# A wider search for the priorities that order the dense stage of an attention, feed-forward and mixture-of-experts kernel

## The chip, the cores and the metric

The kernel runs on one core of a Trainium2 chip. The metric is the device time of one execution in microseconds (us); the figure for a kernel is the median of its runs.

## What is computed

Attention over pooled keys and values, a dense feed-forward layer on its output, and a layer of eight experts that takes each token to one of them or past them all. Cut to what matters:

```python
k_p = k.reshape(B, H, Sp, pool, D).mean(axis=3)          # 8 batches, 8 heads, 576 tokens, 64 wide, pool 8
v_p = v.reshape(B, H, Sp, pool, D).mean(axis=3)
scores = scale * q @ k_p.T; attn = softmax(scores); x = attn @ v_p    # as 4608 tokens x 512
h = x @ w_in; g = h * (1 / (1 + exp(-h))); x = g @ w_out              # 512 -> 2048 -> 512
do_compute = x @ w_skip > 0
e_idx = argmax(x[do_compute] @ w_gate); gate_w = its softmax value
y = gate_w * (relu(xc @ w1[e]) @ w2[e])                               # 512 -> 1024 -> 512, per expert
out[do_compute] = xc + y
```

## The kernel before

The program has two stages on one core. The **dense stage** (`dense`) does attention, the feed-forward layer and the routing for 36 tiles of 128 tokens, in 18 chunks of 256 (j = 0 to 17). Its work is cut into operations with short names, each a few instructions on one engine. For one chunk they are:

- `mm1(j, f)`, f = 0 to 15: 12 matrix products into `psh` (lines 324 to 326); then `th` (tanh on ACT, line 331), `sw` (DVE, line 337), `gh` (ACT, line 341) and `gl` (POOL or DVE, line 346), which make the two halves of the activated block; then `mm2(j, f)`: 6 products into `pso` (lines 356 to 358).
- `ev(j, t)`: `pso` to the SBUF tile `x` (line 365), and `st`: that tile to the output and to the scratch tensor `x2d` (line 371), by SP's queue.
- `dot`: 9 per tile, 18 per chunk, on DVE (line 376): the scores of eight experts and of the skip. `ra` (lines 389 to 397), `rp` (two small products into `psr`, lines 404 and 405), `re`, `rg` (lines 413 to 420) and `rb` (lines 429 to 437) turn them into list positions, `rs` (POOL, line 440) scatters the rows of one tile into the lists in DRAM. `rb` of a chunk needs that of the chunk before.

For chunk 17 the dots and the routing are not in the dense stage but in the next. The dense stage also prepares the **expert stage**, by operations that stand once: `ft` (line 829 on, the first tile's expert and list position, from the counts up to chunk 15), `fi` (line 913, SP reads the first 256 list rows), `l1` and `l2` (line 928, SP loads the first expert's W1 into `room` and W2 into `wb`, four pieces of 512 KB each; `wb` holds the router's weights until the last dot), `ga` (line 962, POOL gathers the 256 tokens from `x2d` by two indirect transfers), `xp` (line 973, PE turns them), `xq` and `xr` (lines 979 and 983, their two halves), `s1h` and `s1l`, `s2h` and `s2l` (lines 944 and 948, the two halves of a quarter of W1 or W2; the first of each pair on ACT, the second on DVE or POOL), `ti` and `tc` (small tables).

The **expert stage** (`experts`) starts with the first 256 listed tokens, whatever comes of chunk 17: eight groups of 12 products into `p` (lines 997 to 999), between which stand the turning of chunk 17's tiles (line 1052), their scores (`psl`, line 1062) and the routing of chunk 17; then products with W2 into `pys` (from line 1036), and then a chain of blocks of up to 256 tokens with its own loads and splits. Its order is written out in the program.

The dense stage's order is not. `schedule` builds it by list scheduling: every operation has a cost per engine, the operations that it needs, and a height, which is its cost plus the largest height of those that need it plus a bonus:

```python
bonus += bonus_of.get(name[0], {}).get(phase(*name), 0.0)
height[n] = min(ops[n][0].values()) + ops[n][4] + max((SIGNAL + height[u] for u in users[n]), default=0)
(_, t, t1, u), n = max((c for c in can if c[0][1] <= t0), key=lambda c: height[c[1]])
```

Of the operations that could start first, the one with the greatest height is issued next, on the engine whose end plus a penalty (`FIRST`, `LATER`, `KEEP`) is earliest. `bonus_of` is a table by kind of operation and phase: 0 to 3 for chunk 0, 1, 2 and later ones, 8 for the last chunk but one, 9 for the last. Every engine runs its instructions in the order in which they were issued.

Of the kernel before, what the change touches and what calls it, by code (L numbers as in the profile page):

```python
# [52 lines left out]
def body(tc, const, q, k, v, w_in, w_out, w_skip, w_gate, w_r, w1, w2, out, x2d, lst, base, nch, nxt):  # L53
# [3 lines left out]
    with ExitStack() as ctx:  # L57
# [392 lines left out]
        def dense():  # L450
            ops, last, st = {}, {}, {}
            bonus_of = {
# [27 lines left out]
            }  # L480
            by_tile = ("q", "sc", "mx", "ex", "ns", "nr", "pt", "pc", "pv", "xh", "xl", "dot")
            by_chunk = ("mm1", "th", "sw", "gh", "gl", "mm2", "ev", "st", "ra", "rp", "re", "rg", "rb", "rs")
# [159 lines left out]
            if nxt:  # L642
# [19 lines left out]
                for c in (0, 1, 2):  # L662
                    op(("s2h", c), {"A": 1.0}, lambda e, c=c: split_hi(S2, W2h, c), [("l2",), ("mm1", z, 2 * c + 9)])
                    op(("s2l", c), {"V": 1.2, "G": 2.45}, lambda e, c=c: split_lo(S2, W2h, W2l, c, e), [("s2h", c)])
            schedule(ops, last)

        def schedule(ops, last):
            unit = {"T": nc.tensor, "A": nc.scalar, "V": nc.vector, "G": nc.gpsimd, "S": nc.sync}
            room_for = dict(a=2, h=2, o=2 * TPC, x2=4, t=2, gh=3, gl=3, tr=2, kv=3, q=2)
            SHARED, APART = ("ns", "mix", "or", "lo", "nr", "vsum", "vput", "gl", "dot", "kput"), ("rs", "ga", "setup", "ti")  # L670
            FIRST = {"V": 0.786439, "G": 0, "A": 0.394171}
            LATER = {"V": 1.58663, "G": 0, "A": -0.769199}
            FILL, HOLD, KEEP = 181.563, 0.9, 0.6
            SIGNAL, SAME, ISSUE, REACH, COLD, IDLE, WARM = 0.135, 0.05, 0.45, 2.0, 1.8, 3.4, 4.0

            def gap(a, b):
# [22 lines left out]
            def earliest(n):  # L699
# [13 lines left out]
                for u, c in cost.items():  # L713
# [17 lines left out]
                    if len(cost) > 1:  # L731
                        more += (LATER if t > FILL else FIRST).get(u, 0.0)
                    if best is None or t + c + more < best[0]:
# [41 lines left out]
        def tiny(shape, dt=F32, parts=1, src="r"):  # L775
            n = 1
            for d in shape:
                n *= d
            o = small[src]
            small[src] = o + n  # L780
            t = (wb if src == "w" else room)[0:parts, o:o + n]
            if dt != F32:
                t = t.bitcast(dt)
            names = "abcd"[:len(shape)]
            return t.rearrange(f"p ({' '.join(names)}) -> p {' '.join(names)}",
                               **{x: d for x, d in zip(names, shape)})
# [10 lines left out]
        ex = tiny([NXP + 1, 1])  # L797
# [408 lines left out]
        with tc.manual_schedule():  # L1206
            setup()
            dense()
            if nxt:
                experts()  # L1210
# [52 lines left out]
```

## Time and profile before

| | before |
|---|---|
| median of 3 runs | 1345.49 us (1344.15 to 1347.27) |
| profiled execution, its own time | 1348.03 us |
| its span, first to last instruction | 1346.3 us |
| mean granted TensorE clock | 0.98 |
| busy: PE, DVE, ACT, POOL | 1270.8, 792.9, 568.6, 580.4 us |

PE runs the matrix products and is busy for 94% of the span. "Busy" of PE is modelled: products overlap, so a row's duration is longer than the distance to the next row. The rest of the profiled execution's time (1348.03 less 1346.3) lies around the span.

### The profile page before, as it was taken

The numbers are of one execution on the slowest core, as the hardware profiler recorded it, in microseconds if no ns is written. First come the engines' busy times: TensorE is split into PE (matmuls) and PEld (weight loads), VectorE is DVE, ScalarE is ACT, GpSimd is POOL, SyncE is SP. The second block draws the span as 40 slices with busy tenths as digits, with TensorE's granted clock in tenths as the row PEclk, the third lists the DMA queues.
The fourth block names the chain that finished last, engine by engine and source line by source line (L and its number), as shares of the span: only waits on it lengthen the run. The fifth ranks groups of instructions, "written<-read, shape, count | busy, mean of one in ns | idle before, by whom it ended". The sixth has DMA issues, their size and how long they took to land. (4 is left out here: it accounts for less than half of the span.)

```text
span 1346.3 us, 24483 instructions
## 1 busy us (share of the span) xinstructions
PE 1270.8 (94%) x8508; PEld 1132.8 (84%) x8508; DVE 792.9 (59%) x2011; ACT 568.6 (42%) x1619; POOL 580.4 (43%) x644
## 2 busy tenths in 40 slices
PE   4999999999999999999999999999559999999895
PEld 3889898898889898888888989989459999999674
DVE  7997782564837647557467547492473222333785
ACT  5876533444344444444444434433131121223573
POOL 3456355345635632663563323422271212133664
PEclk9999999999999999999999999999869999999998
DMA  7653502111301201121111101100141111426661
GB/s 244 203 197 128 198 27 61 40 40 35 92 17 62 88 9 48 58 62 48 58 35 48 40 9 40 40 33 1 45 160 48 58 40 56 166 86 251 235 240 36
DMA packets 51311, 113.84 MB, mean 85 GB/s; under 512 B 12311, under 2 KB 13335, under 8 KB 51024
## 3 DMA queue, kind: packets, MB, share of 16 engines
q1 hardware_dynamic: 44960, 96.39, 21.5%
q0 software_dynamic: 6192, 15.49, 3.5%
q8 instruction: 80, 1.31, 0.4%
q14 instruction: 79, 0.65, 0.2%
HBM read 134.58 MB, written 26.62 MB: 120 GB/s over the span
## 5 line engine op out<-in xcount | busy, mean ns | idle before, releaser
L346 POOL TENSOR_TENSOR gl<-t,gh 128x256 fp32r<-128x256 f32 x278 | 224.8, 809 | 351.9 <-ACT gh L341 247.8
L324 PE MATMUL psh<-xh,w_hi 128*128 128x256 f32 x1152 | 332.3, 288 | 1.9 <-DVE t L337 1.7
L325 PE MATMUL psh<-xl,w_hi 128*128 128x256 f32 x1152 | 323.5, 281 | 0.0
L326 PE MATMUL psh<-xh,w_lo 128*128 128x256 f32 x1152 | 323.0, 280 | 0.0
L376 DVE SCALAR_TENSOR_TENSOR junk<-x,wb 128x512 bf16<-128x512 f32 x306 | 254.7, 832 | 14.8 <-ACT x L365 9.3
L337 DVE SCALAR_TENSOR_TENSOR t<-t,psh 128x256 f32<-128x256 f32 x288 | 119.8, 416 | 210.7 <-ACT t L331 209.9
L356 PE MATMUL pso<-v_hi,gh 128*128 128x512 f32 x576 | 232.7, 404 | 0.0
L324 PEld LDWEIGHTS psh<-xh,w_hi 128*128 128x128 f32 x1152 | 217.8, 189 | 16.0 <-issue 4.7
L358 PE MATMUL pso<-v_hi,gl 128*128 128x512 f32 x576 | 225.1, 391 | 2.0 <-POOL gl L346 2.0
L357 PE MATMUL pso<-v_lo,gh 128*128 128x512 f32 x576 | 226.3, 393 | 0.0
L325 PEld LDWEIGHTS psh<-xl,w_hi 128*128 128x128 f32 x1152 | 217.7, 189 | 7.1
L326 PEld LDWEIGHTS psh<-xh,w_lo 128*128 128x128 f32 x1152 | 217.6, 189 | 0.0
L331 ACT ACTIVATE t<-psh 128x256 f32<-128x256 f32 x288 | 110.9, 385 | 224.8 <-PE psh L326 197.0
L341 ACT CAST gh<-t 128x256 fp32r<-128x256 f32 x288 | 117.0, 407 | 161.5 <-DVE t L337 140.1
L358 PEld LDWEIGHTS pso<-v_hi,gl 128*128 128x128 f32 x576 | 108.2, 188 | 28.1 <-POOL gl L346 2.5
L356 PEld LDWEIGHTS pso<-v_hi,gh 128*128 128x128 f32 x576 | 108.1, 188 | 14.6 <-issue 0.5
L357 PEld LDWEIGHTS pso<-v_lo,gh 128*128 128x128 f32 x576 | 108.4, 188 | 13.1
L1000 ACT ACTIVATE v_hi<-p 128x256 fp32r<-128x256 f32 x88 | 33.5, 384 | 185.8 <-PE p L999 177.5
L274 ACT ACTIVATE room<-pss,mx 128x72 f32<-128x72 f32 x288 | 88.2, 319 | 53.4 <-DVE mx L266 46.6
L285 POOL TENSOR_TENSOR room<-room,sm 128x288 f32<-128x288 f32 x72 | 61.2, 850 | 101.9 <-DVE sm L280 65.9
L997 PE MATMUL p<-xh,w_hi 128*128 128x256 f32 x352 | 102.4, 291 | 2.1 <-ACT xh L979 1.8
L1044 POOL DMA_INDIRECT out_dram<-own,room x27 | 28.2, 1045 | 174.1 <-DVE own L1042 124.6
(189 smaller groups left out, 2236.1 us busy)
## 6 DMA issues: line engine op xcount, KB each, us to landing
more<-in_w_dram SPq DMA_DIRECT2D x72, 512.0 KB
room<-in_w_dram SPq DMA_DIRECT2D x40, 512.0 KB
wb<-in_w_dram SPq DMA_DIRECT2D x36, 512.0 KB
room<-in_k_dram SPq DMA_DIRECT2D x32, 288.0 KB
room<-in_v_dram SPq DMA_DIRECT2D x64, 144.0 KB
room<-in_q_dram SPq DMA_DIRECT2D x36, 256.0 KB
out_dram<-x SPq DMA_DIRECT2D x36, 256.0 KB
x2d<-x SPq DMA_DIRECT2D x36, 256.0 KB
```

Of the source, the lines that this page charges most:

```text
L324: nc.tensor.matmul(out=ps, lhsT=w4_hi[:, f, kk], rhs=xh[:, kk], start=(kk == 0), stop=False)
L325: nc.tensor.matmul(out=ps, lhsT=w4_hi[:, f, kk], rhs=xl[:, kk], start=False, stop=False)
L326: nc.tensor.matmul(out=ps, lhsT=w4_lo[:, f, kk], rhs=xh[:, kk], start=False, stop=(kk == KD - 1))
L331: nc.scalar.activation(out=t, in_=ps, func=ACTF.Tanh, scale=0.5)
L337: nc.vector.scalar_tensor_tensor(out=t, in0=t, scalar=1.0, in1=ps, op0=ALU.add, op1=ALU.mult)
L341: nc.scalar.copy(out=gh, in_=t)
L346: eng.tensor_tensor(out=gl, in0=t, in1=gh.bitcast(F32), op=ALU.subtract)
L356: nc.tensor.matmul(out=ps, lhsT=gh[:, ts], rhs=v_hi[:, f], start=(f == 0), stop=False)
L357: nc.tensor.matmul(out=ps, lhsT=gh[:, ts], rhs=v_lo[:, f], start=False, stop=False)
L358: nc.tensor.matmul(out=ps, lhsT=gl[:, ts], rhs=v_hi[:, f], start=False, stop=(f == NF - 1))
L376: nc.vector.scalar_tensor_tensor(out=junk, in0=x2_t[i], scalar=1.0, in1=wb[:, e * DM:e * DM + DM], op0=ALU.mult, op1=ALU.mult, accum_out=l ...
L997: nc.tensor.matmul(out=ps, lhsT=W1h4[:, kk, m], rhs=xh[:, kk], start=(kk == 0), stop=False)
```

## The change

The numbers of the table `bonus_of` are others, and so are three constants of `schedule`. No operation, cost or dependency is changed; every engine's instructions are the same in kind and nearly in number, since a few `gl` and `nr` go to DVE in place of POOL.

```diff
             bonus_of = {
-                "abs": {0: 99.4}, "k": {0: 562.4, 1: -230.6, 2: -24},
+                "abs": {0: 115.6}, "k": {0: 643.6, 1: -266.5, 2: 119.9},
...
-                "rp": {0: 272.4, 1: -72.3, 2: 244.4, 3: 61.3},
+                "rp": {0: 272.4, 1: -72.3, 2: 263.8, 3: 85, 8: -18.1},
...
-            FIRST = {"V": 0.786439, "G": 0, "A": 0.394171}
-            LATER = {"V": 1.58663, "G": 0, "A": -0.769199}
-            FILL, HOLD, KEEP = 181.563, 0.9, 0.6
+            FIRST = {"V": 0.786439, "G": 0, "A": 0.363077}
+            LATER = {"V": 0.90992, "G": 0, "A": -0.821894}
+            FILL, HOLD, KEEP = 196.057, 0.9, 0.6
```

What it moves is seen in the instructions as they are issued. On PE, at the seam between the two stages, before (`pst` are the transposes of the gathered tokens, `p0` the first group of the expert stage; the last product of the dense stage stands five rows above the first of these, and the first `psr` of chunk 15, not shown, behind it):

```order
L404 LDWEIGHTS triu_94
L404 MATMUL psr_11487<-ohb_11023,triu_94 128x16
L405 LDWEIGHTS ones_95
L405 MATMUL psr_11487<-ohb_11023,ones_95 128x16
L404 LDWEIGHTS triu_94
L404 MATMUL psr_11636<-ohb_11614,triu_94 128x16
L405 LDWEIGHTS ones_95
L405 MATMUL psr_11636<-ohb_11614,ones_95 128x16
L973 MATMUL pst_11658<-ident_62,room_106 128x128 x4
L973 MATMUL pst_11668<-ident_62,room_106 128x128 x4
L997 MATMUL p0_11712<-xh_11679,w_hi_101 128x256
```

And now, between `mm2(17, 12)` and `mm2(17, 13)`:

```order
L357 MATMUL pso_11140<-v_lo_110,gh_11508 128x512
L358 MATMUL pso_11140<-v_hi_103,gl_11512 128x512
L973 MATMUL pst_11606<-ident_62,room_106 128x128 x4
L973 MATMUL pst_11611<-ident_62,room_106 128x128 x4
L404 LDWEIGHTS triu_94
L404 MATMUL psr_11623<-ohb_11556,triu_94 128x16
L405 LDWEIGHTS ones_95
L405 MATMUL psr_11623<-ohb_11556,ones_95 128x16
L356 MATMUL pso_11139<-v_hi_103,gh_11580 128x512
L357 MATMUL pso_11139<-v_lo_110,gh_11580 128x512
L358 MATMUL pso_11139<-v_hi_103,gl_11618 128x512
```

Before, the routing products of chunks 14, 15 and 16 and the turned tokens stood behind all dense products; now those of chunks 14 and 15 stand behind `mm1(17, 4)` and `mm1(17, 6)`, and the rest ahead of the last three `mm2`.

On DVE, before, the dots of chunk 16 (`x_11537` and `x_11539` are its two tiles) behind `ft`, which stands behind the last `sw` of chunk 17 and two `rb`:

```order
L842 CAST room<-room 1x2
L843 COPY room<-room 1x1
L844 TENSOR_TENSOR room<-room 1x8
L376 SCALAR_TENSOR_TENSOR junk,lg<-x_11537,wb 128x512 x9
L376 SCALAR_TENSOR_TENSOR junk,lg<-x_11539,wb 128x512 x9
L389 TENSOR_REDUCE rmx<-lg 128x2
```

And now (`x_11281` is the first of the same two tiles), from the `sw` of f = 7 of chunk 17 on:

```order
L337 SCALAR_TENSOR_TENSOR t<-t,psh 128x256
L376 SCALAR_TENSOR_TENSOR junk,lg<-x_11281,wb 128x512 x3
L337 SCALAR_TENSOR_TENSOR t<-t,psh 128x256
L376 SCALAR_TENSOR_TENSOR junk,lg<-x_11281,wb 128x512 x3
L337 SCALAR_TENSOR_TENSOR t<-t,psh 128x256
L376 SCALAR_TENSOR_TENSOR junk,lg<-x_11281,wb 128x512 x3
L337 SCALAR_TENSOR_TENSOR t<-t,psh 128x256
L376 SCALAR_TENSOR_TENSOR junk,lg<-x_11300,wb 128x512
L346 TENSOR_TENSOR gl<-t,gh 128x256
```

The dots stand between the `sw` of chunk 17, and `rb(15)` and `ft` ahead of them; behind the last dot stand a split of W1 (`s1l`), `ra(16)`, another split, `sw(17, 14)`, `rg(16)`, a `gl`, `rb(16)` and the last `sw`, and the first three splits of W2 behind `xr`.

On POOL, before (`lst<-row,du` are the scatters of chunks 14 and 15, `room<-x2d,room` the gather):

```order
L346 TENSOR_TENSOR gl<-t,gh 128x256 x27
L440 DMA lst<-row,du 36864x4
L829 IOTA room 1x8
L831 IOTA room 1x8
L440 DMA lst<-row,du 36864x4 x3
L962 DMA room<-x2d,room 128x512 x2
L847 IOTA wb 1x18
```

And now:

```order
L440 DMA lst<-row,du 36864x4 x2
L829 IOTA room 1x8
L831 IOTA room 1x8
L346 TENSOR_TENSOR gl<-t,gh 128x256
L440 DMA lst<-row,du 36864x4
L346 TENSOR_TENSOR gl<-t,gh 128x256 x3
L962 DMA room<-x2d,room 128x512 x2
L346 TENSOR_TENSOR gl<-t,gh 128x256 x2
L948 TENSOR_TENSOR w_lo<-room,w_hi 128x1024 x2
L346 TENSOR_TENSOR gl<-t,gh 128x256
```

The gather now stands directly behind `gl(17, 9)`, and two of POOL's splits of W1 ahead of the last but one `gl`. On ACT, `ev(16)` has moved from behind the last `gh` to between `th(17, 6)` and `th(17, 7)`, and the four `s1h` stand ahead of `th(17, 14)`. On SP, the loads of W1 and W2 now stand ahead of the stores of chunk 17. The first 142 operations on PE, up to the second chunk's end, keep their order.

## Rows read from the trace of the kernel before

**Rows 1.** Busy time by stretch, whole kernel (us; clock granted, DMA share, GB/s last)
```profile
960.30:1012.50 52.20, 22.17 (x139) 20.47 (x138) 42.91 (x144) 13.76 (x23) 28.97 (x22) 0.64 0.32 115
...
997.60:1012.50 14.90, 12.89 (x96) 12.68 (x96) 11.32 (x47) 2.58 (x8) 7.37 (x4) 0.88 0.01 2
...
1012.50:1346.30 333.80, 311.12 (x1898) 275.22 (x1896) 148.94 (x200) 110.17 (x190) 110.48 (x77) 0.98 0.37 123
```

**Rows 2.** Timeline of PE at the seam (start, duration, instruction, [idle before, releaser])
```profile
959.92 0.39 PE L356 MATMUL pso<-v_hi,gh 128*128 128x512 f32 x1
...
980.01 0.19 PE L404 MATMUL psr<-ohb,triu 128*128 128x16 bf16 x1 [19.14 <-DVE ohb L397]
...
985.23 2.31 PE L973 MATMUL pst<-ident,room 128*128 128x128 f32 x8 [5.00 <-DMA room<-x2d,room]
...
991.87 0.58 PE L998 MATMUL p<-xl,w_hi 128*128 128x256 f32 x1 [1.92 <-DVE xl L983]
...
998.25 1.85 PE L1062 MATMUL psl<-wr,x2T 128*128 128x9 f32 x16
...
1003.49 0.17 PE L404 MATMUL psr<-ohb,triu 128*128 128x16 bf16 x1 [1.88 <-DVE ohb L397]
...
1009.70 0.28 PE L997 MATMUL p<-xh,w_hi 128*128 128x256 f32 x1
...
1011.11 0.28 PE L997 MATMUL p<-xh,w_hi 128*128 128x256 f32 x1
```

**Rows 3.** Timeline of DVE at the seam
```profile
930.54 0.42 DVE L337 SCALAR_TENSOR_TENSOR t<-t,psh 128x256 f32<-128x256 f32 x1 [2.38 <-ACT t L331]
...
965.28 0.67 DVE L376 SCALAR_TENSOR_TENSOR junk<-x,wb 128x512 bf16<-128x512 f32 x1
...
979.78 0.17 DVE L397 CAST ohb<-oh 128x16 bf16<-128x16 f32 x1
```

**Rows 4.** Timeline of SP's queue and of ACT at the seam
```profile
973.36 0.41 SPq L913 DMA_DIRECT2D room<-lst  x1
...
975.99 2.52 SPq L928 DMA_DIRECT2D room<-in_w_dram  x4
...
960.12 1.29 ACT L365 ACTIVATE x<-pso 128x512 f32<-128x512 f32 x2 [2.30 <-PE pso L358]
...
982.31 1.04 ACT L944 CAST w_hi<-room 128x1024 fp32r<-128x1024 f32 x1 [3.02 <-DMA room<-in_w_dram]
...
989.21 2.99 ACT L944 CAST w_hi<-wb 128x1024 fp32r<-128x1024 f32 x3
```

**Rows 5.** Timeline of POOL at the seam
```profile
956.91 0.74 POOL L346 TENSOR_TENSOR gl<-t,gh 128x256 fp32r<-128x256 f32 x1 [2.06 <-ACT gh L341]
962.71 1.00 POOL L440 DMA_INDIRECT lst<-row,du  x1 [5.06 <-DVE base L430]
...
971.13 0.98 POOL L440 DMA_INDIRECT lst<-row,du  x1 [1.41 <-DMA lst<-row,du]
976.49 1.50 POOL L962 DMA_INDIRECT room<-x2d,room  x1 [4.38 <-issue]
978.29 1.12 POOL L962 DMA_INDIRECT room<-x2d,room  x1 [0.31 <-issue]
...
999.48 3.52 POOL L1078 MEMSET more<- 128x4096 f32 x1
```

**Rows 6.** Page, costliest groups: the dots over the whole kernel
```profile
L376 DVE SCALAR_TENSOR_TENSOR junk<-x,wb 128x512 bf16<-128x512 f32 x306 | 254.7, 832 | 14.8 <-ACT x L365 9.3
```

**Rows 7.** Timelines of DVE and POOL: splits side by side, and one alone
```profile
991.74 5.58 DVE L948 TENSOR_TENSOR w_lo<-wb,w_hi 128x1024 fp32r<-128x1024 f32 x1
...
991.52 4.70 POOL L948 TENSOR_TENSOR w_lo<-wb,w_hi 128x1024 fp32r<-128x1024 f32 x2
...
1263.56 1.21 DVE L948 TENSOR_TENSOR w_lo<-more,w_hi 128x1024 fp32r<-128x1024 f32 x1
```

**Rows 8.** Waits of PE over the whole kernel (in total, times, longest)
```profile
PE pso L358 <- POOL gl L346: 2.0, 1, 2.0
```

46 rows, old and new, of the table bonus_of are left out of this document.

## The prediction

> **What bounds the kernel now.** I read the page first: PE is busy for 94% of the span, so I looked for the stretches where it is not. The busy times by stretch show one large hole, at the seam between the dense and the expert stage: from 960.3 to 1012.5 us PE is busy 22.2 of 52.2 us, at a mean granted clock of 0.64 [rows 1]. The timeline of PE says what stands there [rows 2]. The last dense product starts at 959.92 and ends at 960.31. Then PE waits 19.14 us for DVE (`ohb`, the end of `ra(16)`), 5.00 us for the gathered tokens, and again for their halves, and the first group of the expert stage runs unbroken only from 991.87. In these waits DVE is doing what it could have done earlier: `rb(14)`, `rb(15)`, `ft`, the 18 dots of chunk 16 and `ra(16)`; from the first dot at 965.28 to the end of `ra` at 979.95 it works without a gap [rows 3]. Before that, during chunk 17's products, it idles 2.38 of every 2.80 us [rows 3]. So a few tiny routing products at the end of PE's queue hold up DVE, DVE the scatters, they the gather, and the gather PE.
>
> The work in the hole is small. At full clock a group of 12 products takes 1.41 us (1009.70 to 1011.11), so the eight groups up to 1012.5 take 11.3; the turned tokens took 2.31 at half clock, so 1.2, and chunk 17's tiles as much; the scores 1.85 [rows 2]. That is 15.5 of 52.2 us: **36.7 us are waiting and half clock.** Behind 1012.5 PE is busy 311 of 334 us [rows 1]; that part should move as a block.
>
> **What the change moves.** Nothing is added or removed; each step below is a move.
>
> *PE's routing products* (four `psr` and the two turns) go ahead of dense products. They were PE work before; the cost is that PE now can wait there. *`ev(16)`, `rb(15)`, `ft` and the dots* go into DVE's idle time.
>
> *Is DVE in time?* `sw(17, 6)` was at 930.54 [rows 3]; from there the new order gives DVE, up to the last `sw`: 18 dots, 13.2 us (14.7 less eight small operations of `ra`, about 1.5) [rows 3], plus 2.9 since beside POOL's work a dot takes 0.83 in the mean against 0.67 alone [rows 3, 6]; 43 small operations (two `rb` of 9, `ft` 11, `ra` 8, `rg` 7 or less) at 0.17, 7.3 [rows 3]; ten `sw` at 0.42, 4.2; two `gl`, at most 0.74 each, 1.5 [rows 5]; two splits of W1 at 1.21, 2.4 [rows 7]. Sum 31.5, so the last `sw` ends near 962.0. From `sw` to the end of its `gl` is 1.5 us (930.96 to 932.45, taking the last `gl` 9 periods of 2.80 back) [rows 3, 5], and the last `mm2` takes 2.80 less 1.41, 1.4. End 964.9. Without any wait PE would end at 960.3 plus the turns and routing products, 1.4: 961.7. So the last products wait **3.2 us** for DVE.
>
> *The splits.* DVE's two splits now stand in front of `ra(16)` and the last `gl`, beside two of POOL's. The nearest row is bad: a DVE split that started 0.22 us behind POOL's pair (4.70) took 5.58 against 1.21 alone [rows 7]. So each may cost between 0 and 4.4 us, 0 to 8.7 for both. I take **1.2**, half of one of POOL's: DVE's first split needs the first ACT split, POOL's the one after it, 1.04 later [rows 4], so DVE's goes first; the second meets the middle of a POOL split.
>
> *The gather* must be there when PE comes to the turns, behind `mm2(17, 12)`: three `mm2` ahead of the old end, 956.1. `rb(15)` ends at about 932. Two scatters with a landing between them, 1.0, 1.4 and 1.0 [rows 5], and a handover: 935.7. SP read the list 1.25 us behind the last scatter, and POOL's gather began 3.13 behind that [rows 4, 5]: 940.1. It stands behind `gl(17, 9)`, which ended at 940.85 before (six periods ahead of the last) [rows 5]. From the gather's start to PE's was 985.23 less 976.49, 8.7 [rows 2, 5]: 949.6. Margin 6.5 us, so it costs **nothing**; if it fails, rival 3.
>
> Here a rule speaks against the change. By the rows a scatter beside running dots took 0.98 and one without them 1.00 [rows 5], so I leave POOL's transfers at their durations though they move beside a busy DVE. The Trainium skill (SBUF — State Buffer, the box behind SBUF: two separate sides, and Who interferes with whom) says that a DVE operation in a two-port mode, such as a plain copy, locks GpSimd out of writing descriptors, 620 ns becoming about 3100 in its example. Four transfers in the chain, 2.5 us each, would be 10 us as an estimate by that page.
>
> *The loads.* W1's first piece was used 6.3 us after issue (975.99 to 982.31) [rows 4]. W1 is now issued near 937, needed near 951. W2 must wait for the last dot, near 952: three pieces by about 962, wanted behind `ev(17)` at 966. Nothing, with 4 us of cover.
>
> *Behind the seam.* The first three splits of W2 now stand behind `ev(17)`. Chunk 17's scores need: two `ev` 1.29, three ACT splits 2.99 [rows 4], a DVE split 1.21, an operation of 0.42 and a copy as long as a dot, 0.67: 6.6 us behind the last dense product. PE has two groups and the turning, 4.0. A new wait of **2.6**. Then `ra(17)`: PE waited 1.88 for it before [rows 2], while POOL cleared a buffer for 3.52 [rows 5], which now starts nearer to it; between 0 and 3.5, I take **2.5**. Half clock: before, the mean of 0.88 over 14.9 us [rows 1] means 3.6 us at 1.2 GHz, which lost 1.8; PE still pauses, so **1.8** again.
>
> *The middle.* Chunks 2 to 16 are reordered too. PE's waits there were near nothing before (the longest of its kind, for POOL's `gl`, 2.0 us once, in the first 100 us) [rows 8]; the sum stays, 2 us either way for the range.
>
> **Sum.** 36.7 less 3.2, 1.2, 2.6, 2.5 and 1.8 (11.3) is 25.4 us. The profiled execution took 1348.03 (1346.3 and 1.7 around it): 1322.6. It is 2.5 above the median of 1345.49; by the median, **1320.1 us**.
>
> **The rivals.**
> 1. *The locks are kind.* DVE keeps up, no wait for `ra(17)`, full clock: what remains is 3.2 and 2.6, gain 30.9, 1314.6. For it: DVE's first split starts first. Against: the 1.88 before. Chance 0.09.
> 2. *The splits block DVE* as in the row of 5.58, twice: 8.7 in place of 1.2, gain 17.9, **1327.6**. For it: DVE has no slack left. Against: order of start. Chance 0.13.
> 3. *The gather is late* in front of the last three `mm2`. If DVE's work held each of the four transfers for as long as POOL's held DVE's split, 4.4 us [rows 7], the gather would land 17.5 later, at 967.1, and PE wait 11.0; the 3.2 and 1.2 for DVE would lie inside: **1326.7**. It decides from 1.6 us per transfer, where the margin is used up. Against: 0.98 beside dots. Chance 0.05. The rule of the Trainium skill above is this rival's, and by its figure PE would wait 3.5.
> 4. *Slower:* the new table makes one `mm2` of every chunk wait for its `gl`, as happened once for 2.0 us [rows 8]. For chunks 3 to 16, 14 times 2.0 is 28, which eats the 25.4: 1348. It decides from 1.8 us per chunk. For it: more `gl` on DVE, between dots. Against: not one such wait in the middle before, with the same cost of work. Chance 0.03.
> 5. *The change does not do what it says:* the chain to the gather hangs on something else, and PE stands at the turns instead of behind them: 1345. Against: every link of the chain is in the rows. Chance 0.02.
>
> **How the numbers follow.** The forecast has 0.68; its own spread by the open terms (the locks, the waits behind the seam, the middle) is 1315 to 1326. The range takes in rivals 1 to 3: 1313 to 1329. A change of 0.2%, 2.7 us, is about what a measurement of this kernel can tell from none. Faster: forecast and rivals 1 to 3, 0.95; same, rival 5, 0.02; slower, rival 4, 0.03.
>
> **What would show it.** Right: PE's 19.14 and 5.00 us waits gone; dots of chunk 16 between `sw` of chunk 17, from about 932; the gather about 941 to 945; the last `mm2` ending 963 to 968; groups of the expert stage at once behind it; `pys` from about 987; the rest 334 us long as before. Wrong: a wait of PE for the gather ahead of the last `mm2`; DVE splits of 3 us and more with PE idle behind them; a wait for `x2T` above 5 us; waits for `gl` or `t` in the middle.

## The result, and the profile after

| | before | after |
|---|---|---|
| median | 1345.57 us of 4 runs (1344.15 to 1347.27) | 1325.58 us of 4 runs (1324.50 to 1327.99) |
| profiled execution, its own time | 1348.03 us | 1325.16 us |
| its span | 1346.3 us | 1323.5 us |
| busy: PE, DVE, ACT, POOL | 1270.8, 792.9, 568.6, 580.4 us | 1267.6, 800.7, 570.2, 570.2 us |

The ratio is 0.9852 [0.9837, 0.9867]: the change is faster by 1.5%, that is by 20.0 us by the medians and by 22.8 by the two profiled spans. The forecast was 1320.1, a gain of 25.4, in a range of 1313 to 1329.

The busy times of after by stretch (us; PE, PE's loads, DVE, ACT, POOL; granted clock, DMA share, GB/s), to be read beside [rows 1]: from the turning of the gathered tokens to the end of the dense stage, on to the routing products of chunk 17, to the first `pys` product, and the rest.

```profile
957.09:969.11 12.02, 7.93 (x29) 5.98 (x28) 8.75 (x34) 2.87 (x7) 5.55 (x9) 0.72 0.01 0
969.11:980.83 11.72, 7.51 (x62) 7.10 (x60) 8.72 (x15) 6.18 (x12) 5.80 (x2) 1.00 0.24 90
980.83:989.85 9.02, 8.89 (x63) 8.79 (x62) 7.43 (x36) 1.53 (x4) 1.98 (x2) 0.81 0.02 3
989.85:1323.50 333.65, 310.81 (x1898) 275.27 (x1896) 148.91 (x200) 110.18 (x190) 110.55 (x77) 0.98 0.37 123
```

The last line is the block of 333.80 us of [rows 1]: 333.65, with the same 1898 products. The first `pys` stood at 1012.52 before and stands at 989.85 now, 22.67 earlier, so the whole difference of the spans arises ahead of it. It also arises after 924: the last product of `mm1(17, 4)`, up to which both kernels have done the same number of products of every kind, ended at 924.77 against 924.43. The middle gave nothing. What is left is the seam. PE's timeline there, against [rows 2]:

```profile
957.09 1.03 PE L973 MATMUL pst<-ident,room 128*128 128x128 f32 x8
960.59 0.18 PE L404 MATMUL psr<-ohb,triu 128*128 128x16 bf16 x1 [2.47 <-DVE ohb L397]
...
963.03 0.80 PE L358 MATMUL pso<-v_hi,gl 128*128 128x512 f32 x1 [1.62 <-DVE gl L346]
...
964.90 0.63 PE L356 MATMUL pso<-v_hi,gh 128*128 128x512 f32 x1
965.33 0.63 PE L357 MATMUL pso<-v_lo,gh 128*128 128x512 f32 x1
...
968.88 0.39 PE L358 MATMUL pso<-v_hi,gl 128*128 128x512 f32 x1
969.11 0.28 PE L997 MATMUL p<-xh,w_hi 128*128 128x256 f32 x1
...
973.55 1.06 PE L1062 MATMUL psl<-wr,x2T 128*128 128x9 f32 x8 [0.56 <-ACT x2T L1055]
...
980.83 0.17 PE L404 MATMUL psr<-ohb,triu 128*128 128x16 bf16 x1 [2.89 <-DVE ohb L397]
...
989.85 0.40 PE L1036 MATMUL pys<-w_hi,v_hi 128*128 128x512 f32 x1
```

The wait of 19.14 us has become 2.47, the one of 5.00 for the gathered tokens is gone, and so is the one for their halves: `p` follows the last dense product without a gap (968.88, 969.11). New are 1.62 for the `gl` of the first of the last three `mm2`, two short waits for `x2T` (0.56, and 0.75 at 975.36), and 2.89 in place of 1.88 for chunk 17's `ohb`. And one thing is no wait at all: from 963.62 to 967.89 the dense products stand 0.43 us apart (964.90, 965.33) where the last of them stand 0.23 apart (968.88, 969.11). That is half clock; the granted clock over 964.00 to 969.11 was 0.61.

DVE in the same stretch, against [rows 3] and [rows 7]:

```profile
936.12 0.67 DVE L376 SCALAR_TENSOR_TENSOR junk<-x,wb 128x512 bf16<-128x512 f32 x1
...
937.57 1.41 DVE L376 SCALAR_TENSOR_TENSOR junk<-x,wb 128x512 bf16<-128x512 f32 x1
...
952.95 2.80 DVE L376 SCALAR_TENSOR_TENSOR junk<-x,wb 128x512 bf16<-128x512 f32 x1
955.68 0.08 DVE L376 DVE_READ_ACCUMULATOR junk<-x,wb 128x1 f32 x1
955.68 3.44 DVE L948 TENSOR_TENSOR w_lo<-room,w_hi 128x1024 fp32r<-128x1024 f32 x1
...
960.36 0.17 DVE L397 CAST ohb<-oh 128x16 bf16<-128x16 f32 x1
960.46 1.22 DVE L948 TENSOR_TENSOR w_lo<-room,w_hi 128x1024 fp32r<-128x1024 f32 x1
...
976.87 0.18 DVE L390 TENSOR_TENSOR lg<-lg,rmx 128x16 f32<-128x16 f32 x1
977.08 0.18 DVE L391 SCALAR_TENSOR_TENSOR oh<-lg,rev 128x16 f32<-128x16 f32 x1
...
977.59 2.77 DVE L395 TENSOR_SCALAR cm<-lg 128x2 f32<-128x2 f32 x1
```

And POOL, against [rows 5]:

```profile
932.57 0.96 POOL L440 DMA_INDIRECT lst<-row,du  x1 [2.53 <-DVE t L337]
...
936.17 1.48 POOL L440 DMA_INDIRECT lst<-row,du  x1 [1.58 <-DMA lst<-row,du]
937.66 0.76 POOL L346 TENSOR_TENSOR gl<-t,gh 128x256 fp32r<-128x256 f32 x1
...
944.13 1.04 POOL L962 DMA_INDIRECT room<-x2d,room  x1 [0.56 <-DMA room<-in_w_dram]
945.48 1.21 POOL L962 DMA_INDIRECT room<-x2d,room  x1 [0.31 <-issue]
...
952.78 5.26 POOL L948 TENSOR_TENSOR w_lo<-room,w_hi 128x1024 fp32r<-128x1024 f32 x2 [1.37 <-ACT w_hi L944]
...
976.83 3.50 POOL L1078 MEMSET more<- 128x4096 f32 x1
```

The dots of chunk 16 now run from 936.12, and the gather starts at 944.13, 13 us ahead of PE's turning. Three rows of DVE are far too long for what they are: the last dot (2.80 against 0.67), the split behind it (3.44 against 1.22) and a line-395 operation on two columns (2.77). Each lies beside a long instruction of POOL: the two splits from 952.78 to 958.04, the clearing of a buffer from 976.83 to 980.33. In what follows such a DVE operation is called held. Five more dots took 1.21 to 1.41 us, each beside a `gl` of POOL (0.74 to 0.76), and so cost DVE 2.9 us in all.

### The profile page after: what moved, and what is told of

The parts are those of the page before. It is cut to its first block, busy times and chain, and to the rows that moved or that the text cites. A ratio compares the mean times of both kernels' runs of the same rounds, so it can differ in the third digit from the quotient of the medians.

```text
span 1323.5 us, 24479 instructions
## 1 busy us (share of the span) xinstructions
PE 1267.6 (96%) x8508; PEld 1129.3 (85%) x8508; DVE 800.7 (60%) x2021; ACT 570.2 (43%) x1619; POOL 570.2 (43%) x634
## 5 line engine op out<-in xcount | busy, mean ns | idle before, releaser
L376 DVE SCALAR_TENSOR_TENSOR junk<-x,wb 128x512 bf16<-128x512 f32 x306 | 266.2, 870 | 8.3 <-ACT x L365 2.9
L1001 DVE SCALAR_TENSOR_TENSOR v_hi<-p,v_hi 128x256 fp32r<-128x256 f32 x88 | 36.9, 424 | 109.5 <-ACT v_hi L1000 96.9
L285 POOL TENSOR_TENSOR room<-room,sm 128x288 f32<-128x288 f32 x70 | 58.3, 833 | 101.7 <-DVE sm L280 69.9
```

Of the source, the lines that this page charges most:

```text
L376: nc.vector.scalar_tensor_tensor(out=junk, in0=x2_t[i], scalar=1.0, in1=wb[:, e * DM:e * DM + DM], op0=ALU.mult, op1=ALU.mult, accum_out=l ...
```

## The experiments

Ratios are to the kernel before, run on the same chip; each kernel's medians are in us. The theory at the start: the gain is the seam's chain and nothing else; what is missing from 25.4 is DVE held by POOL. The rivals: part of the gain is the reordering elsewhere, and the holds are covered by other waits.

**One number of the old table.** The smallest change that could move the chain: in the kernel before, the priority of SP's read of the list alone.

```diff
-  "or": {0: -15.2}, "fi": {0: 190.3},
+  "or": {0: -15.2}, "fi": {0: 990.3},
```

> The kernel before with one number of the table raised: the bonus of fi, the read of the first list rows, from 190.3 to 990.3. A bonus raises everything that leads to its operation, so the chain rp(14), rb(14), ev(16), rp(15), rb(15), ft and the dots of chunk 16 is issued earlier; PE's routing products of chunks 14 and 15 stand behind mm1(17, 5), the gather behind gl(17, 10). Theory (only the seam counts, and there only that this chain starts early): most of the gain of the change, 18 to 24 us under the kernel before, 1322 to 1328; PE's first W2 product (pys) from 988 to 995. Rival (the gain needs the whole new table, the order of chunks 2 to 16 too): less than half of the gain, above 1335.

Measured: 1328.48 (1328.15 to 1331.22) against 1347.15, ratio 0.9870 [0.9850, 0.9889]. PE's timeline:

```profile
959.54 1.03 PE L973 MATMUL pst<-ident,room 128*128 128x128 f32 x8
...
983.17 0.17 PE L404 MATMUL psr<-ohb,triu 128*128 128x16 bf16 x1 [8.13 <-DVE ohb L397]
...
992.84 0.39 PE L1036 MATMUL pys<-w_hi,v_hi 128*128 128x512 f32 x1
```

18.7 us come with one number, against the 20.0 of the whole new table (which has 319.1 for `fi`). An operation takes over the height of what needs it, so a high `fi` also pulls up the scatters, `rb(15)` and the routing products, which `fi` needs. What the new table gives beyond that is small: the wait of 8.13 for chunk 17's `psr` is 2.89 in after, and `pys` starts 3.0 earlier.

**The routing products last again.** The changed kernel, but `rp` of chunks 14 to 16 also needs the last dense product, which puts their six products into `psr` back behind it.

```diff
-  ..., lambda e, j=j: route_sum(j), [("ra", j)], ("a", ("rp", j)))
+  ..., lambda e, j=j: route_sum(j), [("ra", j), j > 13 and ("mm2", nch - 1, NF - 1)], ("a", ("rp", j)))
```

> The changed kernel with one dependency more: the routing products of chunks 14, 15 and 16 may only be issued behind the last dense product, as they were before. All other numbers of the new table stay. Theory (the seam's chain is the whole of the gain): back to the time before, 1342 to 1349, with PE waiting about 19 us for ohb. Rival (the new order of the middle gives part of the gain): it stays 5 us or more under the kernel before, at 1340 or less.

Measured: 1346.12 (1345.07 to 1348.12), ratio 0.9995 [0.9986, 1.0004]. PE:

```profile
982.12 0.20 PE L404 MATMUL psr<-ohb,triu 128*128 128x16 bf16 x1 [19.13 <-DVE ohb L397]
986.28 1.08 PE L973 MATMUL pst<-ident,room 128*128 128x128 f32 x4 [3.93 <-DMA room<-x2d,room]
```

The long wait of [rows 2] is back to 0.01 us, and most of the one for the gather, with all numbers of the new table in place; `pys` starts at 1012.62 (1012.52 before). So the gain is the seam's, to within the 1.9 us that the interval leaves open, and it hangs on where a few tiny products stand in PE's queue.

**The clearing later.** The buffer is cleared behind the routing of chunk 17 in place of ahead of it.

```diff
             split(S2, W2h, W2l, 3, nc.gpsimd)
-            nc.gpsimd.memset(stages[1][0], 0.0)
             xm1p(0, 1)
...
             route_b(c)
+            nc.gpsimd.memset(stages[1][0], 0.0)
             xm1p(0, 3)
```

> The changed kernel with POOL's clearing of the buffer more (line 1078) moved behind the routing of chunk 17. Theory (PE's 2.89 us wait for ohb of chunk 17 is the clearing, which holds the operation of line 395 on DVE for 2.77 us): line 395 back to 0.2 us, the wait 0.2 to 0.6, pys and the end 2.0 to 2.6 us earlier, 1323.0 to 1323.6 against the changed kernel's 1325.6. Rival (the wait is the length of the small operations and the copy on ACT): unchanged within 0.5 us.

Measured: 1323.67 (1322.31 to 1327.22), ratio 0.9832 [0.9813, 0.9851]. The line-395 operation took 0.16 us, and PE's wait fell from 2.89 to 0.29. In the profiled execution `pys` started at 985.20, 4.65 ahead of after; 0.67 of it stood already at the turning (956.42). But the rest of the span was longer:

```profile
977.38:985.20 7.82, 7.37 (x63) 7.28 (x63) 7.09 (x34) 1.78 (x6) 3.28 (x3) 1.00 0.02 5
...
985.20:1322.00 336.80, 311.62 (x1898) 275.14 (x1896) 150.95 (x202) 110.35 (x190) 112.83 (x78) 0.98 0.36 122
```

336.80 against 333.65. The hold on line 395 is gone, and so is the half clock behind it (1.00 where after had 0.81). But the clearing, now from 983.89 to 987.43, held another operation: line 887, a copy of 28 numbers in the tables of list positions. In after and here:

```profile
989.71 0.16 DVE L887 COPY room<-wb 1x28 f32<-1x28 f32 x1
```

```profile
985.50 1.96 DVE L887 COPY room<-wb 1x28 f32<-1x28 f32 x1
...
995.40 0.66 PE L973 MATMUL pst<-ident,room 128*128 128x128 f32 x4 [0.65 <-DMA room<-x2d,room]
```

SP reads the next lists 0.6 to 0.7 us behind this copy in both traces (988.05 here, 990.54 in after), and POOL gathers their tokens 2.5 behind that. PE, which came to the next block earlier, waited for the gather (0.65) and behind it twice more (0.78 and 0.41); after has none of these three waits. So most of what the removed hold gave was lost to a new one; the last kernel of this section has the clearing at the same place, but its copy took 0.23, and the rest of its span 333.95 without these waits. By the medians the gain is not shown at all: 0.9832 here and 0.9852 for the changed kernel, with intervals that overlap.

**The splits of W1 on DVE alone.** The scheduler may no longer give POOL a part of the four.

```diff
-  op(("s1l", c), {"V": 1.2, "G": 2.45}, lambda e, c=c: split_lo(S1, W1h, W1l, c, e), [("s1h", c)])
+  op(("s1l", c), {"V": 1.2}, lambda e, c=c: split_lo(S1, W1h, W1l, c, e), [("s1h", c)])
```

> The changed kernel with all four low splits of W1 on DVE, none on POOL. DVE gets two splits of 1.21 us more. Theory (POOL's two splits, 5.26 us, held a dot of DVE for 2.1 us and a split for 2.2, more than DVE needs to do them itself): no dot above 1.5 us, the four splits 1.2 each, the last mm2 ends 3 to 6 us earlier than 969.1, the time 3 to 6 us under the changed kernel, 1320 to 1323. Rival (DVE is full, and two more splits only add to it): 1 to 3 us slower than the changed kernel, 1326.5 to 1328.5.

Measured: 1323.15 (1321.84 to 1323.52), ratio 0.9824 [0.9809, 0.9839]. DVE:

```profile
953.09 0.68 DVE L376 SCALAR_TENSOR_TENSOR junk<-x,wb 128x512 bf16<-128x512 f32 x1
...
953.70 5.17 DVE L948 TENSOR_TENSOR w_lo<-room,w_hi 128x1024 fp32r<-128x1024 f32 x4
```

All four splits take 5.17 us of DVE. With POOL's help the last dot and DVE's two splits took 7.46 (2.80, 3.44 and 1.22), of which 0.67 is the dot's own. The wait for `ohb` fell only to 2.13, but the one for `gl` is gone, and PE's products behind it ran at full clock:

```profile
959.79:961.92 2.13, 0.00 (x1) 0.00 (x1) 1.96 (x8) 1.40 (x4) 2.13 (x6) 1.00 0.00 0
961.92:964.81 2.89, 2.89 (x14) 2.41 (x15) 2.54 (x18) 0.47 (x1) 0.02 (x1) 1.00 0.00 0
```

The dense stage ended at 964.81 in place of 969.11, 4.3 us. Nearly half of that is the shorter waiting (4.09 to 2.13), the rest in the main the half clock that did not come.

**The clearing earlier, and both edits.** First the clearing ahead of the first group of the expert stage; then that with the splits on DVE; beside them the changed kernel once more.

```diff
             stages.append((more[:, 0:KD * F2], more[:, KD * F2:]))
+            nc.gpsimd.memset(stages[1][0], 0.0)
             xm1p(0, 0)
...
-            nc.gpsimd.memset(stages[1][0], 0.0)
             xm1p(0, 1)
```

> The changed kernel with POOL's clearing of the buffer more moved to the other side: ahead of chunk 17's transposes and of POOL's split of W2, right behind the last dense product, where POOL idled 6.37 us. Theory (the clearing costs only through the operation on DVE that it holds, so a place where DVE runs no such operation is free): the wait of 2.89 us for ohb falls to 0.2 to 0.6 us as in the run with the clearing later, without the 2.5 us of small new waits behind it there (gather, halves, DVE's late operations); pys from 985 to 988 and the time 2 to 3 us under the changed kernel of the same call. Rival (the clearing delays the last W2 split, which is needed soon): 1 us of gain or less.

> The changed kernel with both: all four low splits of W1 on DVE, and the clearing of more right behind the last dense product. Theory (two separate locks): the gains add, 3.5 and about 2, so 4.5 to 6.5 us under the changed kernel of the same call, about 1319 to 1321, the lowest of all. Rival (both hide the same wait): no more than the larger of the two, 3.5 to 4.

> The changed kernel once more, on the same chip as the two others, as their base: 0.983 to 0.987 of the kernel before, as measured first.

Measured, with 1346.21 for the kernel before: the clearing earlier 1325.76 (1321.40 to 1327.59), ratio 0.9847 [0.9830, 0.9864]; both 1323.09 (1322.57 to 1323.73), 0.9829 [0.9815, 0.9842]; the changed kernel again 1326.47 (1325.70 to 1327.30), 0.9855 [0.9840, 0.9870]. The first does not decide: its five times fall into 1321.4 and 1322.0 on one side and 1325.8 to 1327.6 on the other, and only the fastest was profiled. In that execution the hold was gone (line 395 took 0.16, PE waited 0.29, `pys` started at 986.45). The second is no better than the splits alone were (0.9824), so the two gains do not add. Its trace shows why, in the stretch of the last dense products, on DVE and on POOL:

```profile
960.52:962.65 2.13, 0.00 (x2) 0.01 (x1) 1.96 (x8) 1.40 (x4) 2.13 (x6) 0.98 0.00 0
962.65:967.07 4.42, 4.42 (x14) 3.53 (x15) 3.10 (x21) 0.49 (x1) 0.64 (x2) 0.62 0.00 0
```

```profile
975.04 2.91 DVE L391 SCALAR_TENSOR_TENSOR oh<-lg,rev 128x16 f32<-128x16 f32 x1
...
978.27 0.16 DVE L395 TENSOR_SCALAR cm<-lg 128x2 f32<-128x2 f32 x1
```

```profile
972.06 3.53 POOL L1075 MEMSET more<- 128x4096 f32 x1
975.55 2.36 POOL L948 TENSOR_TENSOR w_lo<-wb,w_hi 128x1024 fp32r<-128x1024 f32 x1
```

The same wait of 2.13 was followed by half clock this time: 4.42 us for the products that took 2.89. And the hold only changed its place: the clearing, which had to wait for the second scatter, ran from 972.06 to 975.59 and pushed POOL's own split to 975.55 to 977.91, so that line 391 was held in place of line 395 (2.91), and PE waited 3.02.

**The splits on DVE and the clearing later.** The two edits that had each removed a hold, together, with the splits alone and the changed kernel as bases in the same series.

> Changed kernel with the four splits of expert 0's first W1 block on VectorE alone and the clearing of the second staging buffer issued behind the routing of chunk 17. Lock theory: both known holds are gone at once (the 2.8 and 3.44 us on VectorE near 953 and 956, and the 2.7 us in the line-395 operation near 974 to 977), and POOL's own split (2.37 us from about 971) ends before line 391 starts near 973.2, so nothing else steps in. The line-404 product of chunk 17 should then wait under 0.3 us, the first product of line 1036 should start 1.5 to 2.5 us earlier than in the kernel with the splits alone (986.45), and the median should lie 4.5 to 6 us under the changed kernel and 1 to 2.5 under the splits alone. Rival (a hold moved is only exchanged for another wait, as the earlier clearing showed): the line-1036 product again near 986.5 and the median within 1 us of the splits alone.

> The kernel with the four splits on VectorE alone once more, as the base that the run before it is compared with on the same chip. Both theories: 2.5 to 4 us under the changed kernel of the same call; the line-395 operation of chunk 17 held 2.7 us.

> The changed kernel unaltered, as the base of this call. Both theories: 1324 to 1327.5 us, a ratio to the kernel before of 0.984 to 0.987.

Measured, with 1346.76 for the kernel before: both 1321.76 (1318.77 to 1322.10), ratio 0.9806 [0.9790, 0.9822]; the splits alone 1322.26 (1320.98 to 1323.18), 0.9818 [0.9803, 0.9832]; the changed kernel 1326.87 (1325.31 to 1327.62), 0.9850 [0.9836, 0.9865]. Against the changed kernel both edits give 5.1 us and the splits alone 4.6; the two cannot be told apart. In the routing of chunk 17 DVE was held only at line 390, by 0.22 us, and PE no longer waits for it. PE's timeline with both edits:

```profile
975.19 0.41 PE L999 MATMUL p<-xh,w_lo 128*128 128x256 f32 x1
975.41 0.24 PE L404 MATMUL psr<-ohb,triu 128*128 128x16 bf16 x1
975.49 0.18 PE L405 MATMUL psr<-ohb,ones 128*128 128x16 bf16 x1
976.53 0.58 PE L997 MATMUL p<-xh,w_hi 128*128 128x256 f32 x1 [0.86 <-DVE v_hi L1001]
```

and its busy times ahead of and behind that routing product:

```profile
971.30:975.40 4.10, 4.07 (x20) 3.98 (x20) 1.82 (x9) 0.17 (x1) 2.35 (x1) 0.56 0.01 1
975.40:980.00 4.60, 3.73 (x19) 3.64 (x19) 2.28 (x17) 0.87 (x3) 0.99 (x1) 0.50 0.02 5
```

The lock theory was right about the wait (2.44 with the splits alone, none here) and the rival about the time: from the turning of chunk 17's tiles to `pys` it is 19.65 us against 20.28, and `pys` started at 986.15, where 984 to 985 was expected. PE has no wait there but works at a granted clock of 0.56 and 0.50: the products of `p` stand 0.21 apart, where 0.12 is full clock, and the group that would have waited is simply late. Half clock was there with the splits alone too: over 970.60 to 976.99, with the wait in it, the granted clock was 0.73 in this series and 0.54 in the first one. What differs is how long it lasted: the 25 products of `p` behind the routing product took 5.49 us here and 4.59 with the splits alone. So a wait of 2.4 us was exchanged for 0.86 behind `v_hi` and for more products at half clock.

## Why the prediction was right, and where it was off

The mechanism held: the chain from the routing products over DVE, the scatters and the gather to PE was moved ahead of the end of the dense stage, and its two long waits went. The prediction's sum, term by term against the trace of after:

| term | forecast | measured |
|---|---|---|
| dense products wait for DVE, without holds and for holds | 3.2 + 1.2 | 2.47 + 1.62 = 4.1 |
| half clock on the last dense products | 0 | 2.6 |
| PE waits for the gather | 0 | 0 |
| new wait for `x2T` | 2.6 | 0.56 + 0.75 = 1.3 |
| wait for chunk 17's `ohb` | 2.5 | 2.9 |
| half clock behind the seam | 1.8 | 0.19 of 9.02 us = 1.7 |
| remains of the 36.7 | 11.3 | 12.6 |

36.7 less 12.6 is 24.1, where `pys` came 22.7 earlier and the spans differ by 22.8. Of the 1.4 between, 0.3 stood already behind `mm1(17, 4)`, and 0.3 was a misreading: the prediction takes the product at 959.92 for the last dense one of before, but two more follow, so that dense work filled the hole's first 0.3 us.

```profile
960.39 0.39 PE L358 MATMUL pso<-v_hi,gl 128*128 128x512 f32 x1
960.62 0.18 PE L404 MATMUL psr<-ohb,triu 128*128 128x16 bf16 x1
```

The remaining 0.8 is in no row of the table.

- **The step that failed** is the half clock: the sum had it behind the seam alone, though the wait of 3.2 us that it put ahead of the last products could lower the clock for those as well. From 960.59 to 969.11 the two routing products and 18 dense ones took 8.52 less 1.62 of waiting, 6.9 us, where they take 4.2 to 4.3 at full clock (18 at 0.23): 2.6 lost. (Of it 2.0 by the granted clock of 0.61 over the 5.1 us behind 964.00; the rest ahead of that, about the wait, where the product at 963.03 took 0.80.) "The last `mm2` ending 963 to 968" became 969.1 by this. It was no accident of one execution: in the four other profiled executions of the changed order with two splits on POOL, the granted clock of this stretch was 0.59 or 0.60 as well. With all splits on DVE, and so without the second wait, it was 1.00 in three executions of four.
- **The holds were mis-sized**, and that the sum of the waits came out (4.1 for 4.4) was luck. They cost DVE 2.1 on a dot and 2.2 on a split, 4.3 in place of 1.2. The reason given ("DVE's goes first") failed: POOL's first split started at 952.78, 0.17 ahead of DVE's last dot. That dot was in no one's list of victims. The sum of DVE's work was about 1.6 us too large without them (the last `sw` was to end at 962.0 and ended at 964.74 with 4.3 of holds), which hid the error; its 2.9 for dots beside POOL's work is what the five dots beside a `gl` cost. Rival 2 named the mechanism at twice its price.
- **The gather** was in time. It started at 944.13, inside the 941 to 945 of the signs, behind `gl(17, 9)`, which ended at 943.57 in place of 940.85; with the 8.7 us that the prediction took from there to PE, that leaves about 4 of the 6.5 us of margin, by estimate. The second scatter took 1.48 and the gathers 1.04 and 1.21 beside running dots (the first scatter, 0.96, stood ahead of them), so the price that the Trainium skill gives (SBUF — State Buffer, A bandwidth-pool intuition that's wrong (but worth ruling out)) for a transfer overlapped with a DVE copy is not seen with these dots. No copy ran beside the four transfers, so the rule itself was not tried here. Rival 3 did not come.
- **Rivals 4 and 5**: behind the first 120 us one `mm2` of the middle waited for its `gl`, for 0.3 us, and the change does what it says; the second experiment shows that the chain was all, to within 1.9 us.
- **Median and profile.** 25.4 was forecast by the profiled execution, and the spans gave 22.8, a miss of 2.6. The other 2.8 down to the 20.0 of the medians lie in the profiled execution of before, which was 2.5 above its median, and in that of after, 0.4 below. The prediction read the gain off the profiled execution and took it from the median, as if no part of those 2.5 us lay in the hole. Where they lie isn't known; only one execution of each was profiled.

## What to carry to other kernels

A tiny operation on the busiest engine's queue holds up all that hangs on it: look at what the first operation behind a hole needs, and follow it back to the last thing that could have been issued earlier; here one priority gave 18.7 us, where the whole table gives 20. When a wait is removed, price what the engine does next at the clock it will have, not at full clock, and what the helper engine's long instructions will then stand beside: sharing four splits between DVE and POOL cost 4.6 us against leaving them all to DVE. And two such gains need not add, since an instruction of POOL that is moved away from one DVE operation can hold the next: the clearing held line 395, moved back line 887, and moved ahead it pushed a split on to line 391.

## What the runs showed of the hardware

- A DVE operation can last as long as POOL's instruction beside it, whatever its own size. The line-395 operation on 128x2 took 2.77 us and ended at 980.36, POOL's clearing at 980.33; in the kernel before the same line took 1.75, up to the end of the same clearing. With the clearing later, the copy of line 887 on 1x28 took 1.96. Under the clearing the operations of lines 390 and 391, each with two inputs, took 0.18. Beside POOL's split line 391 was held (2.91). The Trainium skill (SBUF — State Buffer, Who interferes with whom) says just this: two SBUF inputs contend with a GpSimd operation that reads and not with one that only writes, while a `tensor_scalar` can enter a two-port mode and contend; whoever issues first keeps the ports for the whole instruction. The traces agree, with two rows left open in which DVE's operation starts first: line 391 in the kernel with the splits on DVE and the clearing earlier starts at 975.04, half a microsecond ahead of the split that held it, while the clearing still ran; and the dot at 937.57 took 1.41, though the `gl` beside it starts 0.09 later.
- The granted clock behind a wait is not decided by the wait's length alone. Behind 2.13 us of waiting at the same place the last dense products ran at 1.00 (2.89 us) in one kernel and at 0.62 (4.42 us) in another; 1.00 is 2.4 GHz, and 0.62 a mix of that and 1.2. PE's instructions ahead were the same in both, 0.7 us apart; two more executions with the splits on DVE had 2.16 and 2.12 us of waiting there and 1.00 behind it. Why it fell in one and not in the other stays open; the two groups of times of the clearing moved earlier may be the same thing, which was not shown.
